# A delta-rule attention with a routed attention behind it, on one core: the first unit's key loads in two pieces, the mask's constants first, 48 small products at the start, and a new order of steps

## The chip, the core and the metric

The kernel runs on one core of a Trainium2 chip. The core has five engines that run side by side, each through its own list of instructions in order: TensorE (PE, matrix products; its weight loads are PEld), VectorE (DVE), ScalarE (ACT), GpSimd (POOL) and SyncE (SP, which here only issues transfers). They wait for one another by semaphores. The metric is the device time of one execution in microseconds (us), from the first to the last instruction, as the median of timed runs.

## The reference

```python
def _attn_ref(q, k, v, beta):                 # 4 batches, 8 heads, 768 tokens, 48 features
    k_n = k / (np.linalg.norm(k, axis=-1, keepdims=True) + 1e-06)
    state = np.zeros((B, H, D, D)); y = np.zeros_like(q)
    for t in range(S):
        kt, vt, bt = (k_n[:, :, t], v[:, :, t], beta[:, :, t, None])
        y[:, :, t] = np.einsum('bhd,bhde->bhe', q[:, :, t], state)
        v_old = np.einsum('bhde,bhd->bhe', state, kt)
        state = state + bt[:, :, :, None] * np.einsum('bhd,bhe->bhde', kt, vt - v_old)
    return y
...
def _moe_ref(x, w_gate, wq, wk, wv, wo):      # x: y as 4 x 768 x 384; 4 experts of width 64, the best 2 count
    logits = x @ w_gate
    ...                                       # w: softmax over the 2 largest logits of a token
    for e in range(E):
        q = x @ wq[e]; k = x @ wk[e]; v = x @ wv[e]
        scores = scale * (q @ k.transpose(0, 2, 1))
        scores = np.where(causal, -1000000000.0, scores)
        a = np.exp(scores - scores.max(-1, keepdims=True))
        a /= a.sum(-1, keepdims=True) + 1e-09
        ye = a @ v @ wo[e]
        ...                                   # out += (w of e, if e is one of the token's two) * ye
```

The recurrence over 768 tokens is the first half, a causal attention of four experts the second.

## The kernel before, in words

The work is cut into six units `n` (two pairs of batches, three thirds of the tokens each). A unit has 256 tokens in four chunks `c` of 64, and eight pairs of heads; the two heads of a pair lie on partitions 0 and 64, the two sides. Units 0 to 2 follow one another for one pair of batches, 3 to 5 for the other.

In a unit each chunk's recurrence becomes a triangular solve. First come the products of K with itself (`gr`, `gram`). `st_in` (`si`) transposes them on DVE, and `pre` (five steps) makes the norms. Then the steps `sv` follow, nearly all of two elementwise instructions: for units 1 to 5 on POOL, 32 steps (L334, L335), for unit 0 on DVE with half the size, 15 steps (L337, L338). `so` and `sn` transpose the result back on DVE. Unit 0's blocks of 16 are then widened to 64 by `dg` (copies on ACT and POOL) and `ex` (four rounds of 32 products for each chunk); its side products are `gu`. Units 1 to 5 widen theirs by `m1`, `mv` and `m2`. `gq` multiplies K and Q, and two DVE instructions copy that out under a mask (L271).

After that each chunk runs a chain: `ks` (K by the state), a subtraction on DVE, `u` (the solved matrix by it), a copy on ACT (L449), `s` (the new state), and for the output `q` and `y`. Pairs of chunks then go through the second half: `hx` (transfers within the core), `pj` and `pv` (projections), `mx`, `mp`, `mr` (row maxima), `sc` (scores and exponentials), `av`, `nm`, `ft`, `fo` (values, output projection, store). `vt` scales V on POOL. `lg`, `lq`, `lc` load K, Q and K/V, `w` loads weights.

The order in which the steps are written is a table, `ORDER`. It lists 854 steps, and each step emits its instructions on all engines at its place; every engine then runs its own part in that order. A number with a plus sign stands for so many fillers: products of zeros on PE, 128 by 256, which nothing reads (`filler`). The products of most steps go to four PSUM banks `pm__66` to `pm__69`, taken in turn, so a step must wait until the bank's last content has been copied out.

At the start PE also runs `MINI` products of 4 columns of zeros, in two records each. The loads are issued by SP in the order of the code: the first K of unit 0, the constants that the first mask needs, the other three K of unit 0, `beta`, the K of unit 1, and so on. A K chunk is 128 rows of 2 KB, of which rows 48 to 63 and 112 to 127 hold zeros and are read by nothing. Transfers take eight semaphores in turn, so the ninth waits until the first has landed.

Of the kernel before, what the change touches and what calls it, by code (L numbers as in the profile page):

```python
# [38 lines left out]
sv0.4 sv0.5 sv0.6 sv0.7 sv0.8 gu1 lc0.1 vt0.1 +16 gu0 sv0.9 vt0.0 ks0.0 +6 gq0.1 +3 gu2 +21 gr1.0 gr1.1 +1 gr1.2
sv0.10 sv0.11 sv0.12 sv0.13 sv0.14 sv0.16 so0 sn0 dg1 si1 pre1.0 gq0.0 lq1.2 dg0 pre1.1 pre1.2 pre1.3 lq1.1 dg2 pre1.4  # L40
sv1.1 +47 ex1.0 +2 gq1.0 ex0.0 kc2 sv1.2 +9 ex1.1 ex0.1 sv1.3 sv1.4 sv1.5 sv1.6 w1 ex2.0 sv1.7 sv1.8 ex1.2 dg3 ex0.2
+7 ex0.3 ex2.1 w3 ex1.3 u0.0 +5 s0.0 gq1.2 w2 sv1.9 sv1.10 ks0.1 y0.0 +1 u0.1 sv1.11 sv1.12 gq0.2 +2 q0.1 s0.1 lc0.2
vt0.2 sv1.13 sv1.14 sv1.15 sv1.16 sv1.17 w0 ex2.2 lc0.3 ex3.0 vt0.3 +6 ex2.3 ks0.2 y0.1 ex3.1 w4 q0.2 sv1.18 u0.2
lq1.3 sv1.19 sv1.20 sv1.21 ex3.2 s0.2 gq0.3 lg2.1 hx0.1.0 ks0.3 sv1.22 sv1.23 sv1.24 lg2.2 sv1.25 lg2.0 y0.2 ex3.3
pv0.0.0 vs1 w5 sv1.26 q0.3 u0.3 lc1.0 gr2.1 gr2.2 y0.3 lg2.3 gr2.3 sv1.27 sv1.28 sv1.29 lq2.1 gr2.0 sv1.30 si2 pj0.0.2
s0.3 hx0.3.0 pj0.0.0 pre2.0 lc1.1 pv0.0.1 pj0.1.0 q1.0 sv1.31 sv1.32 so1 sn1 vt1.0 ks1.0 lg3.0 vt1.1 mv1.3 mv1.0
pj0.1.2 pre2.1 mv1.2 lq2.2 pre2.2 pre2.3 m11.1 m11.0 pv0.1.1 m21.2 +1 m21.0 mv1.1 m21.1 cl1 pre2.4 sv2.1 sv2.2 sv2.3
gq1.1 u1.0 +5 s1.0 sv2.4 mx0.0.0.0 sv2.5 sv2.6 ks1.1 y1.0 u1.1 sv2.7 sv2.8 lc1.2 lq2.0 mx0.0.1.1 q1.1 mp0.0 mx0.1.0.0
s1.1 mr0.0 mx0.1.1.1 vt1.2 mp0.1 ks1.2 y1.1 lc1.3 pv0.1.0 gr3.0 sv2.9 sv2.10 lq2.3 sv2.11 sv2.12 sv2.13 m21.3 u1.2
sv2.14 q1.2 kc0 +1 s1.2 vt1.3 lg3.1 gr3.1 gq2.3 mr0.1 sv2.15 sv2.16 w6 hx1.1.0 sv2.17 +1 sc0.0.1.0 sv2.18 ks1.3 y1.2  # L50
gq1.3 sc0.1.0.0 gt0 sv2.19 q1.3 u1.3 lg3.2 sc0.0.0.0 y1.3 pv1.0.1 lg3.3 gr3.3 s1.3 sv2.20 sv2.21 gr3.2 lc2.0 si3
pre3.0 pv1.0.0 pj1.0.0 vt2.0 pj1.0.2 lq3.0 hx1.3.0 pj1.1.2 sv2.22 sv2.23 vs0 av0.0.3 sv2.24 +3 gq3.0 sv2.25 gq2.1
ks2.0 mx1.0.0.0 sv2.26 sv2.27 pv1.1.1 pre3.1 pre3.2 av0.1.0 sv2.28 pre3.3 av0.0.0 av0.1.1 sv2.29 sv2.30 av0.0.2 sv2.31
sv2.32 av0.0.1 q2.0 mx1.0.0.1 pre3.4 lc2.1 sc0.1.1.0 so2 sn2 sv3.1 pv1.1.0 pj1.1.0 mv2.0 sv3.2 sv3.3 +7 m12.0 m12.1
cl2 nm0.0 +7 m22.0 sv3.4 mx1.1.1.2 vt2.1 av0.1.3 +2 gq2.0 lg4.0 u2.0 sv3.5 mv2.3 sv3.6 mv2.1 lq3.2 lg5.0 mx1.0.1.3
sv3.7 vs2 av0.1.2 s2.0 sv3.8 mx1.1.0.1 ft0.0 ks2.1 m22.1 gq2.2 nm0.1 lg4.1 y2.0 u2.1 sv3.9 mx1.0.1.2 sv3.10 lq3.1
mv2.2 lc2.2 sv3.11 fo0.0.1 mp1.0 fo0.0.0 vt2.2 sv3.12 q2.1 s2.1 sv3.13 m22.2 m22.3 sv3.14 lc2.3 ks2.2 y2.1 sv3.15
sv3.16 sv3.17 ft0.1 mx1.1.1.3 vt2.3 sv3.18 sv3.19 u2.2 mr1.0 q2.2 s2.2 mx1.1.0.0 mp1.1 sc1.0.0.1 sv3.20 sv3.21 sv3.22
gt1 lg4.2 hx2.1.0 fo0.1.1 gr4.2 ks2.3 y2.2 lc3.0 lg4.3 gr4.1 gq3.2 pj2.0.0 q2.3 u2.3 mx2.0.0.0 sv3.23 sv3.24 sc1.0.0.0
y2.3 gr4.3 gr4.0 lc3.1 si4 pre4.0 sv3.25 av1.0.0 av1.0.1 pre4.1 sv3.26 sv3.27 lq4.1 sc1.0.1.0 sc1.0.1.1 pj2.0.2 sv3.28  # L60
pv2.0.1 hx2.3.0 mr1.1 pj2.1.0 sv3.29 sv3.30 pv2.1.1 sv3.31 mx2.0.0.1 lq4.0 av1.0.2 sv3.32 so3 vt3.0 lq3.3 av1.0.3
vt3.1 mv3.3 mv3.1 sc1.1.0.0 sc1.1.0.1 sn3 m13.1 pre4.2 pre4.3 mv3.0 m13.0 ks3.0 cl3 pre4.4 sv4.1 pv2.0.0 sv4.2 sv4.3
sv4.4 av1.1.0 m23.0 m23.1 fo0.1.0 mx2.0.0.2 sv4.5 sv4.6 sv4.7 sv4.8 u3.0 gq4.1 gr5.0 s3.0 pj2.1.2 gq3.1 ks3.1 y3.0
sv4.9 sc1.1.1.0 sc1.1.1.1 lg5.1 sv4.10 u3.1 lc3.2 nm1.0 gq3.3 sv4.11 mv3.2 q3.1 lq4.3 s3.1 mx2.0.1.5 av1.1.1 mx2.0.1.6
mx2.0.1.4 mx2.0.1.7 vt3.2 ks3.2 y3.1 sv4.12 mx2.0.0.3 m23.2 m23.3 sv4.13 sv4.14 ft1.0 sv4.15 pv2.1.0 u3.2 lc3.3 vt3.3
q3.2 lg5.2 mp2.0 mx2.1.1.6 sv4.16 sv4.17 mx2.1.1.5 hx3.1.0 s3.2 av1.1.2 av1.1.3 sv4.18 mr2.0 lq5.0 fo1.0.1 mx2.1.1.4
sv4.19 sv4.20 sv4.21 ks3.3 lg5.3 y3.2 gr5.2 sc2.0.0.2 mx2.1.0.2 sv4.22 q3.3 mx2.1.0.0 sc2.0.0.1 lc4.0 u3.3 sv4.23
# [749 lines left out]
```

## Time and profile before

| | |
|---|---|
| timed runs, median (lowest to highest of 3) | 432.34 us (432.06 to 434.2) |
| the profiled execution, its own time | 431.71 us |
| its span, first to last instruction | 430.0 us |
| PE busy in the span | 406.0 us (94%) |
| POOL busy | 257.2 us (60%) |
| DVE busy | 275.9 us (64%) |
| ACT busy | 202.8 us (47%) |

The profiled execution's own time is 0.6 us under the median of the timed runs. PE's busy time contains the fillers and the small products of zeros; it says how long PE had something in hand, not that the work was useful.

### The profile page before, as it was taken

The page shows a single profiled execution, that of the slowest core. Times are in us where ns is not written, and L with a number is a line of the kernel's source. Part 1 is how long each engine was busy: PE and PEld are TensorE (multiplying, and loading weights), DVE is VectorE, ACT ScalarE, POOL GpSimd, SP SyncE. Part 2 cuts the span into 40 slices and gives each one's busy share as a digit, 9 for nine tenths or more (in the row PEclk, how much of TensorE's full clock was granted, in tenths as well). Part 3 has the DMA queues.
Part 4 walks back from the last instruction along what each step waited for, and adds up shares of the span by engine and source line. Part 5 has one row for each costly group of instructions (what it writes and reads, how often), then busy time and mean ns, then how long its engine had stood idle before and what let it go on. Part 6 is the DMA issues. An engine that isn't in the chain of part 4 may idle for free.

```text
span 430.0 us, 24315 instructions
## 1 busy us (share of the span) xinstructions
PE 406.0 (94%) x10912; PEld 365.6 (85%) x10912; DVE 275.9 (64%) x615; ACT 202.8 (47%) x555; POOL 257.2 (60%) x477
## 2 busy tenths in 40 slices
...
GB/s 252 190 32 99 65 109 174 58 53 109 102 108 40 3 159 121 148 69 5 84 100 117 23 82 6 97 74 57 59 59 42 24 73 47 32 20 22 20 39 74
DMA packets 18967, 32.72 MB, mean 76 GB/s; under 512 B 2864, under 2 KB 9008, under 8 KB 18864
## 3 DMA queue, kind: packets, MB, share of 16 engines
...
## 4 chain that ended last, share of the span: by engine, by line
PE 73%; DVE 13%; POOL 4%; issue 4%; DMA 2%; ACT 1%; SPq 1%; DVEq 0%; ACTq 0%
PE pm__69 L118 15%; PE pm__67 L118 15%; PE pm__68 L118 12%; PE py L118 12%; PE pm__66 L118 11%; PE xu L118 7%; DVE B L278 3%; POOL B L335 2%; POOL tm L334 2%; DVE B L275 1%; DMA kf<-in_kq_dram 1%; DVE tt L355 1%; DVE tn L352 1%; DMA xh<-h 1%; SPq L489 1%
## 5 line engine op out<-in xcount | busy, mean ns | idle before, releaser
L335 POOL TENSOR_TENSOR B<-B,tm 128x30 f32<-128x30 f32 (+9 forms) x150 | 80.7, 538 | 11.8
L334 POOL TENSOR_TENSOR tm<-B 128x30 f32<-128x30 f32 (+9 forms) x150 | 74.1, 494 | 9.9
L642 POOL TENSOR_SCALAR_AFFINE_SELECT at<-at 128x256 f32<-128x256 f32 x48 | 19.1, 409 | 91.8 <-ACT at L640 58.5
L118 PE MATMUL py<-zb 128*128 128x256 bf16 (+1 forms) x256 | 27.1, 264 | 2.7 <-DVE h L483 1.6
L156 POOL TENSOR_TENSOR kv<-kv,nt 128x384 f32<-128x384 f32 x24 | 19.9, 832 | 14.9 <-DVE B L338 11.2
L118 PE MATMUL py<-qf,sb 48*48 48x64 f32 x704 | 24.8, 218 | 2.9 <-issue 1.9
L118 PEld LDWEIGHTS py<-qf,sb 48*48 48x48 f32 x704 | 21.3, 120 | 6.0 <-issue 2.7
L397 POOL COPY tt<-tt 32x256 f32<-32x256 f32 x40 | 15.7, 392 | 11.4 <-DVE tt L355 10.0
L480 ACT ACTIVATE xh<-py 112x384 fp32r<-112x384 f32 x24 | 11.8, 492 | 19.7 <-PE py L118 19.6
L118 PEld LDWEIGHTS <-zb 128*128 128x128 bf16 x176 | 16.5, 103 | 5.2 <-DVE zb L123 1.1
L449 ACT ACTIVATE ub<-xu 128x384 f32<-128x384 f32 x24 | 11.9, 495 | 18.2 <-PE xu L118 13.0
L587 DVE TENSOR_REDUCE mx<-pm__66 128x1 f32<-128x512 f32 (+3 forms) x28 | 17.3, 617 | 4.7 <-PE pm__67 L118 3.2
L118 PE MATMUL pm__67<-xh,wqkh 128*128 128x256 f32 x108 | 19.9, 284 | 0.0
L587 DVE TENSOR_REDUCE mx<-pm__67 128x1 f32<-128x512 f32 (+3 forms) x25 | 16.0, 640 | 5.8 <-PE pm__68 L118 5.8
L482 DVE TENSOR_TENSOR xh<-py,xh 112x384 fp32r<-112x384 f32 x24 | 13.3, 553 | 8.8 <-ACT h L481 8.8
L461 DVE TENSOR_TENSOR sb<-sb,xu 112x384 f32<-112x384 f32 x20 | 11.0, 550 | 10.4 <-PE xu L118 10.3
L118 PE MATMUL pm__67<-kf 48*64 48x64 f32 (+2 forms) x304 | 12.0, 245 | 5.7 <-issue 4.9
L118 PE MATMUL xu<-xs,tt 64*64 64x48 f32 x768 | 16.7, 221 | 0.5 <-DVE xs L443 0.5
L118 PEld LDWEIGHTS xu<-xs,tt 64*64 64x64 f32 x768 | 14.0, 134 | 3.5 <-issue 1.7
L118 PEld LDWEIGHTS pm__67<-xh,wqkh 128*128 128x128 f32 x108 | 16.5, 188 | 0.3 <-DVE QLO L515 0.2
L278 DVE STREAM_TRANSPOSE B<-tt 32x1024 f32<-32x1024 f32 x8 | 16.4, 2045 | 0.2
L118 PEld LDWEIGHTS pm__67<-kf 48*32 48x32 f32 (+1 forms) x304 | 9.6, 140 | 7.7 <-issue 5.5
(359 smaller groups left out, 1621.6 us busy)
## 6 DMA issues: line engine op xcount, KB each, us to landing
...
```

Source lines behind the costliest of these rows:

```text
L118: T.matmul(o, lhsT=a, rhs=b, start=start, stop=stop, skip_group_check=True)
L156: G.tensor_tensor(vt, vt, PR[n]["nt"][:, c * NP:c * NP + NP, None].to_broadcast([128, NP, HD]), op=OP.mult)
L278: V.transpose(B[r:r + 32], gf[r:r + 32, :, 0:32].rearrange("p t j -> p j t"))
L334: e.tensor_tensor(tv, bc(Z[:, i:i + 1, i + 1:]), bc(Z[:, 0:i, i:i + 1]), op=OP.mult)
L335: e.tensor_tensor(Z[:, 0:i, i + 1:], Z[:, 0:i, i + 1:], tv, op=OP.add)
L397: G.tensor_copy(o[r:r + 32, :, 0:32], o[r:r + 32, :, 32:64])
L449: S.activation(eight(UB), PX, AF.Copy)
L461: V.tensor_tensor(eight(new), eight(state(n, c)), SP, op=OP.add)
L480: S.activation(hi, Y[:, :, 0:3], AF.Copy)
L482: V.tensor_tensor(lo, Y[:, :, 0:3], hi, op=OP.subtract)
L587: V.tensor_reduce(dst.rearrange("p (y x) -> p x y", x=2)[:, x, y:y + per], P[x], axis=AX.X, op=OP.max)
L642: G.affine_select(d, d, pattern=[[0, 2], [1, 128]], compare_op=OP.is_ge, fill=0.0, base=0, channel_multiplier=-1)
```

## The change

Four edits, and a new table.

1. The four K chunks of unit 0 are loaded as two transfers of 48 rows each, one a side, without the rows of zeros. SP issues the transfer of side 0 and ACT that of side 1. All other K chunks are loaded as before.
2. The 32 columns of constants that the first mask reads (`kmask`, columns 208 to 239) are a transfer of their own behind the first K; the other 208 columns of that block come after `beta`. The first ACTIVATE (`one`) stands behind the loads of unit 0.
3. `MINI` is 48, not 40.
4. `ORDER` is another order of the same 854 steps, with 166 fillers instead of 175.

```diff
-MINI = 40
+MINI = 48
...
 ORDER = """
-+2 gr0.0 +4 gr0.2 gr0.3 gr0.1 si0 pre0.0 lq1.0 pre0.1 pre0.2 kc1 pre0.3 pre0.4 sv0.1 +4 gr1.3 cb sv0.2 sv0.3 gu3 kc3
...
++11 gr0.0 gr0.1 +4 gr0.3 gr0.2 si0 cb pre0.0 pre0.1 gu1 lq1.0 pre0.2 pre0.3 pre0.4 vt0.0 sv0.1 sv0.2 sv0.3 sv0.4 sv0.5
...
-    S.activation(one, ZB[:, 0:1], AF.Exp)
+
     def load_k(n, c):
         LD[n, c] = KR[(n * CH + c) % KB]
-        nc.sync.dma_start(LD[n, c], kq[n, c][:, 0:NP * 64])
+        if n:
+            nc.sync.dma_start(LD[n, c], kq[n, c][:, 0:NP * 64])
+            return
+
+        for q, r in ((nc.sync, 0), (nc.scalar, 64)):
+            q.dma_start(LD[n, c][r:r + HD], kq[n, c][r:r + HD, 0:NP * 64])
...
     load_k(0, 0)
-    nc.sync.dma_start(cst[:, 0:240], consts[:, 0:240])
+    nc.sync.dma_start(cst[:, 208:240], consts[:, 208:240])
     for c in range(1, CH):
         load_k(0, c)
+    S.activation(one, ZB[:, 0:1], AF.Exp)
     nc.sync.dma_start(bta, beta)
+    nc.sync.dma_start(cst[:, 0:208], consts[:, 0:208])
```

The first place of which the prediction speaks is the start of SP's list. Before, a K chunk is one row (`kf_114` to `kf_117` are unit 0's chunks 0 to 3, `kf_118` is unit 1's first); what an instruction waits for stands in brackets, DMAHW being the transfers' semaphores.

```order
L143 DMA kf_114<-in_kq_dram 128x512
L166 DMA cst<-in_consts_dram 128x240
L143 DMA kf_115<-in_kq_dram 128x512
L143 DMA kf_116<-in_kq_dram 128x512
L143 DMA kf_117<-in_kq_dram 128x512
L169 DMA bta<-in_beta_dram 128x192
L143 DMA kf_118<-in_kq_dram 128x512
```

The same place of the change; here `kf_122` to `kf_125` are unit 0's chunks 0 to 3. ACT's list begins with the other half of each of these four.

```order
L148 DMA kf_122<-in_kq_dram 48x512
L171 DMA cst<-in_consts_dram 128x32
L148 DMA kf_123<-in_kq_dram 48x512
L148 DMA kf_124<-in_kq_dram 48x512
L148 DMA kf_125<-in_kq_dram 48x512 [waits DMAHW0_49]
L175 DMA bta<-in_beta_dram 128x192 [waits DMAHW1_49]
L176 DMA cst<-in_consts_dram 128x208 [waits DMAHW2_49]
L144 DMA kf_126<-in_kq_dram 128x512 [waits DMAHW3_49]
```

SP's half of chunk 3 is the ninth transfer and so waits until one of the first has landed; before, the ninth was unit 1's third chunk.

The second place is DVE behind unit 0's solve. Before, `so0` (`tt_154`) and `sn0` (`tn`) are followed at once by unit 1's `si1` (`B_182`) and `pre1`, with one `gq` (two rows `pm`) in between.

```order
L355 STREAM_TRANSPOSE tt_154<-B_181 128x32x32
L352 STREAM_TRANSPOSE tn<-B_181 128x32x32
L275 STREAM_TRANSPOSE B_182<-tt_155 128x1024
L291 COPY ss<-B_182 128x32
L292 TENSOR_SCALAR g_701<-ss 128x32
L293 TENSOR_SCALAR g_701<-g_701 128x32
L271 TENSOR_TENSOR pm<-pm__69,cst 128x256
L271 TENSOR_TENSOR pm<-pm__66,cst 128x256
L297 RECIPROCAL rr<-g_701 128x32
```

In the change two `gq` (of `gq1.0` and `gq0.3`) stand ahead of `si1` (`B_195`), and a third (`gq0.1`) behind it.

```order
L362 STREAM_TRANSPOSE tt_167<-B_194 128x32x32
L359 STREAM_TRANSPOSE tn<-B_194 128x32x32
L278 TENSOR_TENSOR pm<-pm__67,cst 128x256
L278 TENSOR_TENSOR pm<-pm__68,cst 128x256
L278 TENSOR_TENSOR pm<-pm__69,cst 128x256
L278 TENSOR_TENSOR pm<-pm__66,cst 128x256
L282 STREAM_TRANSPOSE B_195<-tt_168 128x1024
L278 TENSOR_TENSOR pm<-pm__67,cst 128x256
L278 TENSOR_TENSOR pm<-pm__68,cst 128x256
L298 COPY ss<-B_195 128x32
```

The pair of `gq0.1` stood before inside unit 0's solve, between its ninth and tenth step. On PE, `gq0.1` now stands behind 56 fillers and directly ahead of 3 fillers and the first expansion, `ex1.0`; before, 47 fillers stood ahead of `ex1.0`.

## Rows read from the trace of the kernel before

**Rows 1.** Windows: busy us (instructions) of each engine, granted clock, DMA share, GB/s.

```profile
core 0: us, PE busy (x) PEld busy (x) DVE busy (x) ACT busy (x) POOL busy (x), PEclk, DMA share, GB/s
0.00:35.00 35.00, 28.00 (x897) 21.84 (x899) 24.57 (x67) 15.95 (x51) 10.65 (x27) 1.00 0.52 173
...
200.00:425.00 225.00, 222.51 (x5463) 204.27 (x5457) 130.41 (x309) 114.95 (x312) 108.69 (x200) 1.00 0.18 53
...
75.00:80.00 5.00, 5.00 (x121) 4.88 (x110) 2.63 (x3) 2.63 (x8) 4.21 (x13) 0.66 0.10 21
```

**Rows 2.** Timeline of the first 12 us: start, us, engine, instruction, idle before.

```profile
0.82 0.39 SPq L143 DMA_DIRECT2D kf<-in_kq_dram  x1
...
1.14 1.81 PE L118 MATMUL py<-zb 128*128 128x256 bf16 x83 [1.14 <-DVE zb L123]
...
6.85 0.18 PEld L118 LDWEIGHTS pm__69<-kf 48*32 48x32 f32 x5 [1.71 <-DMA kf<-in_kq_dram]
...
7.59 0.23 PEld L118 LDWEIGHTS pm__67<-kf 48*32 48x32 f32 x8
...
9.53 0.18 PEld L118 LDWEIGHTS pm__69<-kf 48*32 48x32 f32 x5
```

**Rows 3.** The K tiles to 30 us: time from issue to landing, eight loads.

```profile
DMA to landing us min/median/max: 2.9/5.2/6.3
```

**Rows 4.** The chain that ended last, to 110 us: start, us, what.

```profile
17.71 3.30 PE py L118 x16
...
29.55 5.24 PE py L118 x47
34.79 1.08 PE pm__67 L118 x32
...
39.90 0.93 PE pm__68 L118 x32
...
47.45 0.45 PE xu L118 x28
...
72.61 2.08 issue
```

**Rows 5.** Timeline of DVE, from unit 0's products to unit 1's `so`.

```profile
10.94 1.90 DVE L275 STREAM_TRANSPOSE B<-tt 128x1024 f32<-128x1024 f32 x1
...
23.13 0.42 DVE L271 TENSOR_TENSOR pm<-pm__67,cst 128x256 f32<-128x256 f32 x1
23.47 0.41 DVE L271 TENSOR_TENSOR pm<-pm__68,cst 128x256 f32<-128x256 f32 x1
...
27.42 2.04 DVE L355 STREAM_TRANSPOSE tt<-B 128x1024 f32<-128x1024 f32 x1
29.35 1.91 DVE L352 STREAM_TRANSPOSE tn<-B 128x1024 f32<-128x1024 f32 x1
...
33.04 0.39 DVE L291 COPY ss<-B 128x32 f32<-128x32 f32 x1
...
37.40 0.19 DVE L305 SCALAR_TENSOR_TENSOR nn<-rr,bta 128x32 f32<-128x32 f32 x1
...
40.05 0.69 DVE L379 TENSOR_TENSOR VS<-tt,pm__67 128x512 f32<-128x512 f32 x1 [1.69 <-PE pm__67 L118]
...
87.85 2.08 DVE L355 STREAM_TRANSPOSE tt<-B 128x1024 f32<-128x1024 f32 x1
```

**Rows 6.** Timeline of POOL: `dg` copies, unit 1's solve from L308 to L348.

```profile
32.63 0.39 POOL L364 COPY VS<-tn 32x256 f32<-32x256 f32 x1
...
37.74 2.35 POOL L308 TENSOR_TENSOR B<-B,nn 128x1024 f32<-128x1024 f32 x1 [1.25 <-DVE aa L312]
...
48.30 0.30 POOL L363 MEMSET tt<- 32x256 f32 x1
...
82.88 0.24 POOL L348 COPY B<-aa 128x32 f32<-128x32 f32 x1
```

**Rows 7.** Timeline of ACT: the copies behind `u4.0` and `u4.3`.

```profile
264.69 0.53 ACT L449 ACTIVATE ub<-xu 128x384 f32<-128x384 f32 x1
...
305.21 0.49 ACT L449 ACTIVATE ub<-xu 128x384 f32<-128x384 f32 x1 [1.95 <-issue]
```

More of the change, by code (lines that the diff above doesn't have):

```diff
@@ L37 @@
 ORDER = """
-+2 gr0.0 +4 gr0.2 gr0.3 gr0.1 si0 pre0.0 lq1.0 pre0.1 pre0.2 kc1 pre0.3 pre0.4 sv0.1 +4 gr1.3 cb sv0.2 sv0.3 gu3 kc3
[L39 to L67, printed above, removed]
@@ L88 @@
-fo5.0.1 ft5.1 +12 fo5.1.0 fo5.1.1
++11 gr0.0 gr0.1 +4 gr0.3 gr0.2 si0 cb pre0.0 pre0.1 gu1 lq1.0 pre0.2 pre0.3 pre0.4 vt0.0 sv0.1 sv0.2 sv0.3 sv0.4 sv0.5
+sv0.6 sv0.7 sv0.8 +11 gr1.2 sv0.9 +14 gr1.1 sv0.10 gu3 gu0 +5 gu2 kc3 lc0.1 vt0.1 gr1.3 sv0.11 sv0.12 sv0.13 sv0.14
+sv0.16 so0 sn0 +3 gr1.0 dg1 gq1.0 gq0.3 dg0 si1 +56 gq0.1 +3 ex1.0 pre1.0 pre1.1 pre1.2 dg2 +10 ex0.0 pre1.3 dg3 gq0.0
+lq1.2 pre1.4 +9 ex0.1 sv1.1 sv1.2 sv1.3 sv1.4 sv1.5 ex1.1 ks0.0 +1 ex0.2 w4 ex2.0 sv1.6 ex3.0 ex0.3 sv1.7 w5 w1 ex2.1
@@ new lines @@
+sv1.8 sv1.9 sv1.10 u0.0 ex1.2 sv1.11 s0.0 ex1.3 ks0.1 y0.0 lc0.2 vt0.2 lg2.1 sv1.12 sv1.13 ex2.2 lq1.1 sv1.14 sv1.15
+lg2.0 u0.1 q0.1 s0.1 w2 +6 ks0.2 kc1 sv1.16 ex2.3 y0.1 lc0.3 ex3.1 vt0.3 gr2.1 w3 q0.2 u0.2 w0 +5 s0.2 hx0.1.0 sv1.17
+gq0.2 lg2.2 ks0.3 sv1.18 sv1.19 sv1.20 ex3.2 sv1.21 y0.2 sv1.22 sv1.23 sv1.24 sv1.25 +1 ex3.3 kc2 q0.3 vs0 pv0.0.0
+gr2.0 u0.3 gq1.2 y0.3 lg2.3 gr2.3 w6 sv1.26 vs1 gr2.2 s0.3 si2 pj0.0.0 hx0.3.0 pj0.0.2 sv1.27 sv1.28 pv0.0.1 lc1.0 kc0
+sv1.29 sv1.30 pre2.0 +1 pj0.1.0 q1.0 sv1.31 lc1.1 sv1.32 so1 vt1.0 ks1.0 vt1.1 mv1.3 mv1.2 sn1 pre2.1 pj0.1.2 pv0.1.1
```

62 lines of the change are left out of this document (42 added, 20 removed).

## The prediction

> **What bounds the kernel now.** I read the windows first, to see where PE has no room. From 200 us on it is busy 222.5 of 225 us: whatever is late or early there is PE's own queue, and a shift that reaches this stretch comes out at the end at full size. In the first 35 us it is busy 28.0 us, and much of that is fillers [rows 1]. So the change can win ahead of 200 us only, and it touches the first 35 us most. Then I read the timelines of the start. PE waits for K: the second group of products of unit 0 starts at 6.85 us, after a wait for the transfer [rows 2]. DVE can transpose those products at 10.94 us and from there runs unit 0's solve almost without a pause, to `so0` at 27.42 and `sn0` at 29.35 us [rows 5]. Last the chain: up to 34.79 us it runs through fillers, 47 of them in one piece from 29.55 us, and then the first expansion `ex1.0` begins [rows 4]. Its data were there earlier: the last copy that it needs, POOL's second of `dg1`, ended at 32.63 + 0.39 = 33.02 us [rows 6]. So 1.8 us of those fillers are too many. From the expansions the chain goes on PE to unit 0's first chain product at 47.45 us [rows 4], and unit 1's `so1` on DVE at 87.85 us comes 4.7 us after POOL had solved unit 1, at 82.88 + 0.24 = 83.12 us [rows 5, 6]. DVE was behind in its list by then, and the last entry ahead of `so1` copies out a projection of PE. Up to there the pace is PE's, not POOL's.
>
> **The start (edits 1, 2, 3).** PE's first 83 products (80 records of small ones, three of full size) take 1.81 us, to 2.95 us [rows 2]. A full one costs 3.30/16 = 0.206 us at the slower level of PE's clock (256 columns in that time is 1.2 GHz) and 5.24/47 = 0.111 us at the faster [rows 4]; so a small record is (1.81 - 3 x 0.206)/80 = 0.015 us, and the 16 more of edit 3 cost 0.24 us. Nine more fillers ahead of the first products, at the slow level, cost 1.85 us. PE is there at 5.04 us. The first K, issued at 0.82 us, had landed after 2.9 us, at 3.7 us [rows 2, 3], and is smaller now, so nothing waits. A group of a chunk's products takes 7.59 - 6.85 = 0.74 us; three groups and four fillers later, at 8.1 us, the fourth begins. From the fourth group to the transpose it was 10.94 - 9.53 = 1.41 us [rows 2, 5]. The transpose then stands at 9.5 us, 1.45 us earlier. Bounds: at the fast level of the clock from the start it would be 1.5 us earlier still (13 fillers, 0.095 each, and part of the groups). On the other side, SP's half of chunk 3 is the ninth transfer and leaves only when the first has landed, at 3.7 us. With the shortest landing it is there at 6.6 us, before its group (7.3 us); with the longest, 6.3 us [rows 3], at 10.0 us, which puts the transpose at 12.2 us, 1.2 us later than before. I take no wait, because a quarter of the bytes ahead of it is gone and the constants that used to go in between are a seventh. ACT's four issues hide: it does nothing else before 12 us that anyone waits for.
>
> **Unit 0's solve to the expansions (edit 4).** The pair of `gq0.1` leaves the solve: 2 x (23.47 - 23.13) = 0.68 us [rows 5]. `so0` comes 2.1 us earlier, `sn0` ends at 29.1 instead of 31.26 us, and the copies of `dg1` at 30.9. `gq0.1` on PE needs the banks of `gq1.0`, which DVE empties right behind `sn0`, at 29.8 us; its 32 records take no longer than an expansion's 32, 0.93 us [rows 4], and three fillers 0.33 us. So `ex1.0` begins at about 31.0 instead of 34.79 us: 3.8 us. Here 2.1 us come from the earlier solve and the rest from fillers that no longer overrun. For PE's own list this is late enough: 92 fillers and eleven groups from 8.9 us on end at 8.9 + 92 x 0.111 + 11 x 0.74 = 27 us, or 31 us if the first 40 run at the slow level.
>
> **Expansions to the first chain.** DVE is now the one that is late: from 29.1 us it runs two pairs for `gq` (1.36), `si1` (1.90), a third pair (0.68), `pre1` (33.04 to 37.59 before, less the pair within: 3.87) and a fourth pair (0.68), and reaches the first subtraction of an expansion at 37.7 us, against 40.05 us [rows 5]. PE has `ex0.1` ready at 36.8 us (ex1.0, 10 fillers, `ex0.0`, `gq0.0`, 9 fillers) and would reach `ex0.2`, which needs that subtraction, at 37.9 us; it waits until 38.4. Five expansions at 0.93 us bring `u0.0` to 43.1 us. Before, 47.3: **4.2 us earlier**. This is the sum's main term; of it DVE already takes 0.5 us back.
>
> **POOL.** Unit 1's solve starts when `nn` is there, at 37.0 instead of 37.74 us, only 0.7 us earlier. But the four copies of `dg3` stood inside the solve (48.30 us on) and stand ahead of it now: 2 x (0.30 + 0.39) = 1.4 us. So the solve ends at 81.0 us [rows 6], and `so1`, shifted with PE by 4.2 us, is wanted at 83.65. POOL keeps 2.6 us of room, and unit 2's solve gets PE's whole shift.
>
> **The rest of the order.** Behind `u0.3` there are 27 fillers instead of 39, 1.3 us less. I count nothing for them: the ones that went stood where PE waits for unit 2's solve, and a wait takes their place. The last 12 fillers stay. The useful products are the same, and from 200 us on the shift stays what it is.
>
> **The sum.** 431.71 - 4.2 = 427.5 us for the profiled execution, and 0.6 us more for the median of timed runs: **428.1 us**.
>
> **The rivals.** *The shift is eaten on the way* (no change, 430.2 to 434.5). One way: somewhere before 100 us PE waits for a solve, and then only POOL's 2.1 us count; another pause like the 2.08 us at 72.61 us, after which the granted clock is 0.66 from 75 to 80 us (1.7 us lost at half level) [rows 1, 4], leaves 0.4 us: 431.9 us. For it: the fillers before `gq0.1` may run out 2.8 us before DVE frees the bank. Against: one such pause is in the kernel before too. Another way is the split: if the halves of chunk 3 land in 6.3 us, DVE starts 1.2 us late, `so0` comes at 28.0 us, and the first expansion gains 1.1 us by the overrun alone: 431.2 us. The Trainium skill speaks for this one (DMA: Bandwidth & Descriptors, "Rules for kernel authors"): two transfers to disjoint halves of the partitions share the same engines, so splitting a load gains nothing. By that rule the pieces only add transfers that take turns at the semaphores; no row here shows a split load, and against it stands that the rows of zeros could go in no other way.
>
> *Slower* (over 434.5 us): unit 4's chain. In the new table `u4.0` stands later, and between it and `u4.3` stand 35 steps with products instead of 45, some 30 us of PE's work instead of 40 (the sums of these steps' durations in the trace). The chain takes turns with DVE, ACT and POOL; before, it was spread over 305.21 - 264.69 = 40.5 us [rows 7]. If it needs all of that, PE stands 10.5 us in a stretch that has no room: 438.6 us. It decides from a wait of 6.4 us on. Against it: 40.5 us was the spacing of the old table, and unit 0's chain began at 47.45 us and was at its fourth chunk before the pause at 72.61 us [rows 4], some 8 us a chunk.
>
> *More than forecast* (under 425 us): the 1.3 us of fillers and the 1.7 us of slow clock come out as well: 425.1 us and less.
>
> **How the numbers follow.** Forecast (425 to 430.2): 0.56. More: 0.08. Eaten: 0.22. Slower: 0.14. A measurement of this kernel tells 0.5% (2.2 us) from no change. So faster 0.64, same 0.22, slower 0.14. The range leaves out the slower rival and the far end of more: 424.5 to 434.5 us. The forecast's own range is 425 to 430.2 us.
>
> **What would show it.** Right: DVE's first transpose at 9 to 10 us, `so0` at 25 to 26 us, the first expansion at 30.5 to 31.5 us, the first subtraction at 37 to 38.5 us, `u0.0` at 42.5 to 44 us, `so1` before 84.5 us, and PE over 98% busy from 195 us on. Wrong at the start: PE idle in front of chunk 3's products. Wrong in the middle: a granted clock under 1 between 25 and 45 us, or DVE reaching `so1` at once behind POOL. Wrong in the end: gaps of PE between `u4.0` and `u4.3`. What would make the number wrong most easily is a wait between 85 and 200 us, where the whole order is new and I have priced it as before.

## The result: 1.1% slower, and the profile after

| | before | after |
|---|---|---|
| timed runs, median (lowest to highest) | 432.96 us (432.06 to 434.2, 4 runs) | 439.61 us (436.58 to 440.9, 4 runs) |
| ratio to before, 95% interval | | 1.0108 [1.0064, 1.0152] |
| the profiled execution, its span | 431.71, 430.0 us | 436.58, 434.7 us |

The forecast was 428.1 us, with a range of 424.5 to 434.5. The ratio on record is not the quotient of the two medians, which is 1.015; how it was formed is not part of the record. The profiled execution is the fastest of the four after, so its trace shows 4.7 us of loss in the span where the medians differ by 6.7. Runs more than 1.5% above the fastest of their kernel count as slow and are left out of the ratios; the traces of e1 and h3 further down are of such runs.

Windows of the kernel after, against [rows 1]; the last is a stretch at half clock:

```profile
0.00:35.00 35.00, 28.64 (x931) 22.51 (x935) 21.90 (x63) 13.10 (x44) 9.15 (x22) 1.00 0.40 130
200.00:425.00 225.00, 221.87 (x5422) 202.52 (x5417) 132.77 (x321) 113.84 (x310) 109.69 (x201) 1.00 0.17 51
...
95.64:105.88 10.24, 9.35 (x284) 8.57 (x282) 6.82 (x14) 2.98 (x8) 8.50 (x17) 0.50 0.25 81
```

The landing of unit 0's halves of K, against [rows 3], the timeline of PE at the fourth group of products (`gr0.2`), against [rows 2], and the first piece of the chain that has no cause, against [rows 4]:

```profile
DMA to landing us min/median/max: 2.7/3.3/4.8
```

```profile
12.82 0.21 PE L118 MATMUL pm__66<-kf 48*32 48x32 f32 x1 [3.49 <-issue]
```

```profile
9.33 3.49 issue
...
28.78 0.70 issue
29.48 5.18 PE py L118 x46
...
35.72 1.08 PE pm__69 L118 x32
```

K was there, as forecast: SP's last half was issued at 3.7 us, and PE's waits up to 14 us name no transfer of K. But inside `gr0.2`, with nothing to wait for that the profile names, PE stands for 3.49 us. DVE, against [rows 5] (its lines are now 7 higher: L282 is `si`, L362 `so`, L386 the subtraction), and POOL, against [rows 6]:

```profile
13.23 0.29 DVE L257 TENSOR_TENSOR tt<-pm__69,cst 128x128 f32<-128x128 f32 x1 [3.95 <-PE pm__66 L118]
...
13.75 1.94 DVE L282 STREAM_TRANSPOSE B<-tt 128x1024 f32<-128x1024 f32 x1
...
29.66 1.98 DVE L362 STREAM_TRANSPOSE tt<-B 128x1024 f32<-128x1024 f32 x1
...
41.85 0.69 DVE L386 TENSOR_TENSOR VS<-tt,pm__69 128x512 f32<-128x512 f32 x1 [0.40 <-PE pm__69 L118]
...
87.66 2.08 DVE L362 STREAM_TRANSPOSE tt<-B 128x1024 f32<-128x1024 f32 x1
```

```profile
34.82 0.39 POOL L371 COPY VS<-tn 32x256 f32<-32x256 f32 x1
...
42.02 2.37 POOL L315 TENSOR_TENSOR B<-B,nn 128x1024 f32<-128x1024 f32 x1
...
86.11 0.24 POOL L355 COPY B<-aa 128x32 f32<-128x32 f32 x1
```

So DVE begins 2.8 us later than before instead of 1.45 earlier, `so0` comes at 29.66, `ex1.0` at 35.7, and `u0.0` at 47.53 us (47.23 before by the same view, the timeline of PE; 43.1 forecast). The late solve is not all of it: the data of `ex1.0` were there at 34.82 + 0.39 = 35.21 us, and PE came 0.44 us later, straight out of its own products and fillers.

Yet that is not the loss either. When DVE transposes unit 3's solution (`so3`), the two kernels are nearly level (before, then after):

```profile
195.99 2.04 DVE L355 STREAM_TRANSPOSE tt<-B 128x1024 f32<-128x1024 f32 x1
...
195.83 2.05 DVE L362 STREAM_TRANSPOSE tt<-B 128x1024 f32<-128x1024 f32 x1
```

By equal work PE is then 0.9 us behind (an estimate, from the sum of the steps' usual durations in the traces). Most of the 4.7 us come later. From unit 3's first `m1` product to the start of its second `s` (`s3.1`) the kernel before takes 17.03 us (198.41 to 215.44), the one after 22.02 (198.03 to 220.05). By the same estimate 2.1 us more of products stand in that stretch in the new table, and 2.9 us are lost. Of these the windows show 1.5 us as idle time of PE; the rest is spread over steps that take longer than usual there. Windows of before, then of after:

```profile
200.00:210.00 10.00, 10.00 (x305) 9.23 (x298) 3.67 (x14) 6.91 (x16) 8.96 (x17) 1.00 0.08 25
210.00:220.00 10.00, 10.00 (x399) 9.07 (x398) 8.26 (x18) 4.29 (x13) 9.00 (x18) 1.00 0.42 136
```

```profile
200.00:210.00 10.00, 9.48 (x282) 8.79 (x276) 9.00 (x29) 6.83 (x16) 9.00 (x16) 1.00 0.01 4
210.00:220.00 10.00, 9.04 (x247) 7.64 (x241) 8.00 (x21) 3.41 (x10) 6.95 (x14) 1.00 0.22 70
```

DVE is busy 9.00 us of ten instead of 3.67. Its timeline after shows with what: the gates of unit 1 (`gt1`, L548 to L565) and `nm1.0` (L668 to L672) stand there now, and behind them the copies (L278) that free the banks for PE. Nearly half of the time of `gt1` is one small instruction, `gd`, which ends 0.03 us behind a multiplication on POOL, the first row here (`pre4.4`).

```profile
204.30 2.38 POOL L315 TENSOR_TENSOR B<-B,nn 128x1024 f32<-128x1024 f32 x1
204.44 2.27 DVE L549 TENSOR_TENSOR gd<-lg,gm 128x16 f32<-128x16 f32 x1
...
209.63 0.74 DVE L672 TENSOR_TENSOR on<-os,rs 128x512 f32<-128x512 f32 x1
210.30 0.36 DVE L319 TENSOR_TENSOR aa<-rr,bta 128x32 f32<-128x32 f32 x1
210.57 0.41 DVE L278 TENSOR_TENSOR pm<-pm__69,cst 128x256 f32<-128x256 f32 x1
```

PE waited for that copy, in the table of waits from 199 to 212 us:

```profile
PE pm__69 L118 <- DVE pm L278: 0.9, 1, 0.9
```

Between 250 and 270 us both kernels stand, in different places. The one after stands 0.83 us at 262.23, for a copy behind `so4`, and 0.37 at 270.01, for an instruction behind `gt2` and `nm2.0`; the one before stands 1.41 us at 251.28, for a copy behind `pre5.1`. Where the last 0.9 us of the 4.7 are lost these rows don't show. The rival that I had for slower, unit 4's chain, is not it. From the copy behind `u4.0` to that behind `u4.3` it now takes 30.2 us, against 40.5 in [rows 7]:

```profile
277.55 0.49 ACT L456 ACTIVATE ub<-xu 128x384 f32<-128x384 f32 x1 [0.36 <-PE xu L118]
...
307.79 0.49 ACT L456 ACTIVATE ub<-xu 128x384 f32<-128x384 f32 x1 [1.67 <-PE xu L118]
```

### The profile page after: what moved, and what is told of

Same layout as the page of the kernel before. It is cut to its first block, busy times and chain, and to the rows that moved or that the text cites. A ratio compares the mean times of both kernels' runs of the same rounds, so it can differ in the third digit from the quotient of the medians.

```text
span 434.7 us, 24380 instructions
## 1 busy us (share of the span) xinstructions
PE 410.6 (94%) x10919; PEld 370.1 (85%) x10919; DVE 276.4 (64%) x615; ACT 203.6 (47%) x555; POOL 257.6 (59%) x477
## 3 DMA queue, kind: packets, MB, share of 16 engines
q1 hardware_dynamic: 18688, 30.52, 22.3%
## 4 chain that ended last, share of the span: by engine, by line
PE 76%; DVE 13%; issue 4%; POOL 2%; ACT 2%; DMA 1%; SPq 1%; DVEq 0%; ACTq 0%; POOLq 0%
PE pm__68 L118 15%; PE pm__67 L118 15%; PE pm__66 L118 13%; PE pm__69 L118 13%; PE py L118 12%; PE xu L118 7%; DVE B L285 2%; DVE mx L594 1%; DVE B L282 1%; DVE tn L359 1%; PE pm__69 L681 1%; DMA xh<-h 1%; SPq L496 1%; DVE g L300 1%; POOL B L342 1%
## 5 line engine op out<-in xcount | busy, mean ns | idle before, releaser
L118 PE MATMUL py<-zb 128*128 128x256 bf16 (+1 forms) x263 | 26.2, 261 | 3.4 <-DVE h L490 1.6
L118 PE MATMUL pm__68<-xh,wqkh 128*128 128x256 f32 x144 | 27.2, 288 | 0.0
L404 POOL COPY tt<-tt 32x256 f32<-32x256 f32 x40 | 15.8, 395 | 12.2 <-DVE tt L362 4.0
L118 PEld LDWEIGHTS pm__68<-xh,wqkh 128*128 128x128 f32 x144 | 21.9, 188 | 0.6
L594 DVE TENSOR_REDUCE mx<-pm__69 128x1 f32<-128x512 f32 (+3 forms) x28 | 17.5, 627 | 5.5 <-PE pm__66 L118 3.1
L118 PE MATMUL pm__68<-xh,wqkl 128*128 128x256 f32 x72 | 20.1, 279 | 0.0
L594 DVE TENSOR_REDUCE mx<-pm__67 128x1 f32<-128x512 f32 (+3 forms) x20 | 12.1, 606 | 11.4 <-PE pm__68 L118 9.9
L118 PE MATMUL xu<-xs,tt 64*64 64x48 f32 x768 | 17.9, 226 | 0.4
L594 DVE TENSOR_REDUCE mx<-pm__66 128x1 f32<-128x512 f32 (+3 forms) x27 | 16.7, 618 | 1.9 <-PE pm__67 L118 1.9
L118 PE MATMUL xu<-sb,kf 48*64 48x48 f32 x704 | 15.7, 226 | 2.2 <-issue 1.1
L118 PEld LDWEIGHTS xu<-sb,kf 48*64 48x64 f32 x704 | 13.0, 138 | 4.8 <-DVE sb L468 2.1
L456 ACT ACTIVATE ub<-xu 128x384 f32<-128x384 f32 x24 | 11.9, 494 | 10.7 <-PE xu L118 9.0
```

Source lines behind the costliest of these rows:

```text
L118: T.matmul(o, lhsT=a, rhs=b, start=start, stop=stop, skip_group_check=True)
L404: G.tensor_copy(o[r:r + 32, :, 0:32], o[r:r + 32, :, 32:64])
L456: S.activation(eight(UB), PX, AF.Copy)
L594: V.tensor_reduce(dst.rearrange("p (y x) -> p x y", x=2)[:, x, y:y + per], P[x], axis=AX.X, op=OP.max)
```

## The experiments

Two things were to be told apart: the start (with its pause), and the new order behind it. Each ratio is against runs of the kernel before on the same chip; times in us are of the profiled execution. "351st" is when PE starts its 351st product, "m1 to s" the stretch from unit 3's first `m1` to `s3.1`. The medians of the kernel before were 433.0 to 435.9 us on the chips of these runs, 0.7% apart; late times of two traces can therefore differ by about 1 us without any edit (an estimate: 0.7% of 196 us is 1.4 us). Diffs show parts of lines where a line of the table is long.

| kernel | ratio [95%] | 351st | si0 | ex1.0 | u0.0 | m1 to s |
|---|---|---|---|---|---|---|
| before | 1 | 14.65 | 10.94 | 34.72 | 47.23 | 17.0 |
| after | 1.0108 [1.0064, 1.0152] | 12.82 | 13.75 | 35.65 | 47.53 | 22.0 |
| e1_mini24 | 1.0232 [1.0179, 1.0286] | 14.31 | 10.27 | 37.87 | 49.74 | 22.4 |
| e2_loads_only | 1.0070 [1.0036, 1.0103] | 14.29 | 10.59 | 37.38 | 49.89 | 17.0 |
| e3_order_only | 1.0173 [1.0121, 1.0226] | 13.35 | 14.28 | 35.57 | 47.57 | 22.0 |
| e4_start_oldtail | 1.0093 [1.0057, 1.0128] | 14.14 | 10.60 | 38.27 | 50.15 | 17.0 |
| f1_mini48_alone | 1.0163 [1.0104, 1.0223] | 13.15 | 13.92 | 38.22 | 50.73 | 17.0 |
| f2_short_opening | 1.0263 [1.0205, 1.0322] | 13.60 | 10.92 | 37.04 | 48.91 | 24.8 |
| f3_oldstart_newtail | 1.0249 [1.0193, 1.0305] | 14.23 | 11.72 | 35.73 | 48.24 | 22.0 |
| f4_newstart_oldtail | 1.0215 [1.0163, 1.0268] | 13.14 | 14.07 | 36.26 | 48.43 | 17.1 |
| g1_mini32 | 0.9977 [0.9939, 1.0014] | 14.85 | 11.00 | 34.18 | 46.69 | 17.1 |
| g2_31_fillers | 0.9965 [0.9937, 0.9993] | 15.46 | 12.56 | 33.75 | 47.26 | 17.1 |
| g3_mini48_31_fillers | 1.0038 [1.0007, 1.0070] | 13.03 | 13.80 | 35.70 | 48.43 | 17.0 |
| g4_short_opening_16_fillers | 1.0142 [1.0095, 1.0189] | 14.46 | 11.24 | 32.48 | 44.48 | 22.3 |
| h1_fillers_in_waits | 1.0145 [1.0101, 1.0188] | 12.89 | 13.76 | 35.48 | 47.36 | 22.6 |
| h2_newstart16_oldtail | 1.0122 [1.0084, 1.0160] | 13.47 | 9.97 | 31.21 | 43.20 | 17.7 |
| h3_mini43 | 1.0042 [1.0006, 1.0078] | 14.24 | 9.85 | 37.31 | 49.83 | 17.0 |
| h4_mini44 | 1.0092 [1.0056, 1.0128] | 13.43 | 14.00 | 36.85 | 49.36 | 17.0 |
| i1_31_fillers_no_single | 0.9952 [0.9931, 0.9973] | 15.63 | 11.44 | 34.86 | 47.37 | 17.0 |
| i2_mini32_31_fillers_no_single | 1.0072 [1.0036, 1.0108] | 15.76 | 11.87 | 34.08 | 46.99 | 20.0 |

**The opening (e1), and the parts alone (e2, e3).** e1 is the kernel after with one number changed:

```diff
-MINI = 48
+MINI = 24
```

> The kernel after with 24 opening py products instead of 48, nothing else. In the kernel before TensorE stands 2.77 us with no wait (11.87 to 14.65 us, inside gr1.3), in the one after 3.49 us (9.33 to 12.82, inside gr0.2), both times at about the 350th matmul of the program. Theory A (the stall sits at a place of the instruction stream, and the longer opening moved it into the first unit's last K product): with 48 records fewer gr0.2 ends before 9.6 us, si0 starts before 10.0 (13.75 in the kernel after), u0.0 at 43.7 to 44.5 (47.5); a stall of about 3 us comes some 48 records later, in or behind gu1. The total then gains 2 to 4 us, 433 to 438, if the rest of the order costs what it did. Theory B (the stall comes from K, the banks or the clock): it stays inside gr0.2 and si0 stays at 13 us or later; total 438 to 441. If the start is mended and the total stays at 438 or more, the order behind the start holds most of the loss.

The pause moved to `gu1`, as theory A had it, and DVE began at 10.27 us; but `ex1.0` came 2.2 us later than in the kernel after. Its data were there at 31.5 us (POOL's second copy of `dg1`); PE's own list, 56 fillers in it, held it until 37.9. Theory A was right on the pause and wrong on what follows from it.

e2 is before with the new loads (edits 1 and 2; the diff shows the first); e3 is after with the old loads.

```diff
...
-        nc.sync.dma_start(LD[n, c], kq[n, c][:, 0:NP * 64])
+        if n:
+            nc.sync.dma_start(LD[n, c], kq[n, c][:, 0:NP * 64])
+            return
+
+        for q, r in ((nc.sync, 0), (nc.scalar, 64)):
+            q.dma_start(LD[n, c][r:r + HD], kq[n, c][r:r + HD, 0:NP * 64])
...
```

> The kernel before with the changed loads alone (K's halves by two queues without zero rows, the mask's constants ahead); 40 opening products and the old order. Theory A (loads harmless, the loss is of the order and of where the stall falls): the 350th record stays inside gr1.3, si0 starts 1 to 2.5 us earlier than before's 10.94, total 430 to 433. Rival (two queues and the earlier DMA issues on ScalarE cost later work, or the halves land late): total 435 or more. If the old order cannot use the earlier start, 432 to 434 and u0.0 within 0.5 us of before's 47.3.

> The kernel before with the new order and 48 opening products, K loaded whole with its zero rows by one queue as before. Theory A: the stall of about 3 us still falls at the 350th record, inside gr0.2 or near it, si0 at 13.5 to 14.5 as in the kernel after, and the total is that of the kernel after, 437 to 441: the loads bought nothing because the stall ends later than any chunk of K lands. Rival (the new loads carry the loss): 434 or less. If K's later arrival adds to the stall instead of lying beside it: si0 at 15 or later, 441 to 444.

In the old order the loads do not gain: `ex1.0` is 2.7 us later than before, and the total 0.7% longer. PE waited 1.72 us for the last chunk's ninth transfer (to 8.36 us), but that isn't what made `ex1.0` late, for DVE still began 0.35 us earlier than before. Inside the solve DVE then stood 2.91 us for the products of `gq0.1`, to 25.73 us; in h3, which has the old loads, it stands there for 2.78. With the new order and the old loads (e3) `u0.0` comes at 47.57 us, with the new ones at 47.53: up to there the loads bought nothing.

**Where PE pauses (f1, h3, h4).** The windows count PE's products, as records of the trace: a product of `MINI` and most others leave two, a filler one. Up to the pause and up to its end, for the kernel after:

```profile
0.00:9.36 9.36, 7.89 (x350) 5.84 (x351) 1.63 (x7) 2.49 (x4) 6.02 (x16) 1.00 0.60 180
0.00:12.80 12.80, 7.89 (x350) 5.84 (x351) 1.63 (x7) 2.49 (x4) 6.02 (x16) 1.00 0.66 203
```

and for the kernel before, where the pause lies in `gr1.3`, of which nobody is in need:

```profile
0.00:11.90 11.90, 7.65 (x350) 5.26 (x350) 3.08 (x10) 1.49 (x2) 6.01 (x16) 1.00 0.80 266
0.00:14.60 14.60, 7.65 (x350) 5.26 (x350) 5.54 (x17) 1.79 (x3) 6.01 (x16) 1.00 0.85 288
```

Both stop at 350 products, with quite different work. Unit 0's four K groups end at product 343 before and at 368 after. f1 changes the opening alone, h3 and h4 are one product of the opening apart, two records (groups ending at 349 and 351):

```diff
-MINI = 40
+MINI = 48    # f1; h3: 43; h4: 44
```

> The kernel before with 48 opening products for 40, nothing else (edit 3 alone). In all six traces so far TensorE pauses at the same counts of matmuls, 223 and 350 (then 605, 732, 859), whatever stands there, and each pause ends 1.2 to 1.6 us after a transfer of 16 KB on the instruction queue has landed. Theory A (its instructions come in blocks of 127 matmuls, and a block that it reaches too early is waited for): in the kernel before unit 0's four K groups end at count 343, with 48 openings at 359, so the last nine products of gr0.1 wait for the block behind 350. si0 starts at 12.5 to 14.5 us (10.94 before), u0.0 at 48 to 50 (47.3), total 1 to 3 us more than before. Rival (16 small products cost only their own 0.24 us, and the stall belongs to gr1.3 or to the loads): si0 within 0.5 us of 10.94, total within 0.5 us of before.

> The kernel before with 43 opening products for 40. Unit 0's four K groups end at count 349, one ahead of the block end at 350. Block theory: si0 within 0.8 us of before's 10.94 or up to 12.6 as it varied (10.9 to 12.6 in four runs of that start), no pause inside gr0.1, total within 0.7% of before. Rival (the cost grows with each product of the opening): si0 and the total a third of the way to the kernel with 48, that is +1 us and +2.5 us.

> One opening product more than 43: the K groups end at count 351, so the last product of gr0.1 stands behind the block end at 350. Block theory: a pause of 2.5 to 4 us in front of that one product, si0 at 13 to 14.3, 2 to 3 us later than with 43, total 2 to 7 us over the one with 43. Rival: no more than 0.3 us later than with 43 at si0 and in total.

Timeline of h3, then of h4: the product of PE behind the pause, and DVE's `si0`.

```profile
14.24 0.80 PE L118 MATMUL py<-zb 128*128 128x256 bf16 x3 [4.54 <-issue]
...
9.85 1.90 DVE L275 STREAM_TRANSPOSE B<-tt 128x1024 f32<-128x1024 f32 x1
```

```profile
13.43 0.21 PE L118 MATMUL pm__66<-kf 48*32 48x32 f32 x1 [3.67 <-issue]
...
14.00 1.97 DVE L275 STREAM_TRANSPOSE B<-tt 128x1024 f32<-128x1024 f32 x1
```

With 43 the pause falls on a filler, with 44 on the last K product: 4.15 us at `si0` for one product of 4 columns. That shows that the count sets the place. All 20 traces pause at 350 (0.85 to 4.78 us), and none starts its 351st product before 12.82 us (12.82 to 15.76). But the totals of h3 and h4 aren't clearly apart (1.0042 and 1.0092, intervals that overlap; 2 to 7 us were expected). `ex1.0` comes at 37.31 and 36.85, with its data there at 34.61 and 35.95 us: what PE still has to do behind the pause, fillers included, sets it, not the solve. f1 has the same `si0` as h4 and costs more, 1.6%: its `u0.0` is 1.4 us later, the rest comes behind.

**The count behind the start (g1, g2, g3).** g1 is the control with 32 opening products (`MINI`); g2 takes 16 of the 47 fillers out; g3 does so with 48 opening products, so that all later products have the numbers that they had before.

```diff
-+47 ex1.0
++31 ex1.0
```

> The kernel before with 32 opening products for 40: the control for the 48 alone. Unit 0's K groups end at count 327, the block behind 350 again begins inside gr1.3. Theory A (what matters is that the K groups stay ahead of count 350): si0 within 0.6 us of 10.94, u0.0 within 1 us of 47.3, total within 0.7% of before. Rival (any change of the count is as bad, since all 85 block ends behind it then fall on other products, or the shorter opening costs clock): 438 us or more.

> The kernel before with 31 fillers for 47 ahead of the first expansion. The data of ex1.0 are there at 33.0 us, TensorE reaches it at 34.79. Theory (TensorE's fillers set the first expansion): ex1.0 at 33.0 to 33.3, u0.0 at 45.3 to 46.2 (47.3 before), and the total 1 to 2 us lower than before if nothing behind takes it back. Rival (the 16 products fewer move every later block end, and the waits at 50 to 75 us with the clock behind them come out otherwise): total within 1 us of before or over it, though u0.0 is earlier.

> The kernel before with 48 opening products and 31 fillers for 47: the 16 products more at the start are taken out ahead of ex1.0, so that behind it every block of instructions ends where it did in the kernel before. si0 at 13 to 14.5 as with 48 alone. Theory 1 (of the loss of 48 alone the part behind the start is the shift of the later block ends): ex1.0 at 36 to 36.7, u0.0 at 48.5 to 49.5, total 1 to 3 us over before. Theory 2 (the part behind the start comes from the late start itself, waits and clock): total 5 us or more over before, as with 48 alone.

Eight opening products fewer change nothing, so it is not every change of the count that costs. g2 is 0.35% faster, though its pauses fell worse and `u0.0` is where it was; why isn't shown. g3 takes three quarters of f1's loss back (1.0163 to 1.0038): `u0.0` 2.3 us earlier, the rest behind it. Whether that rest is the realigned count or the earlier start isn't separated by these runs.

**A mended start (f2, g4), and the two halves crossed (f3, f4, e4, h2).** f2 brings the K groups of the kernel after back to 343; g4 cuts its fillers too; h2 puts the old sequence behind g4's `u0.0`.

```diff
-MINI = 48
+MINI = 40
...
-+11 gr0.0
++2 gr0.0
...
-si1 +56 gq0.1
+si1 +16 gq0.1    # g4 and h2
```

> The kernel after with 40 opening products for 48 and 2 leading fillers for 11: unit 0's K groups end at count 343 again, ahead of 350; loads and the rest of the new order stay. Theory A: no pause of 3 us inside gr0.2, the one at 223 stays; si0 at 10 to 11 us (13.75 in the kernel after). If the solve is what sets the first expansion, u0.0 at 44 to 45 us. If TensorE's own list does (its fillers, slower while its clock is low, as with 24 openings), ex1.0 at 35 us or later though its data are there by 32.5, and u0.0 at 47 to 50: the start then brings nothing, and the total stays at 436 to 441.

> The kernel after with 40 opening products, 2 leading fillers for 11 (as in the short opening before) and 16 fillers for 56 ahead of gq0.1 and ex1.0. With the short opening alone the data of ex1.0 were there at 32.4 us and TensorE came at 37.04. Theory (TensorE's own list of fillers set the first expansion there): ex1.0 at 32.5 to 34, u0.0 at 44 to 45.8, the earliest of all runs. If the early start holds to the end, total 4 us under the short opening (446) or better. If the sequence behind and the half clock hold the loss: u0.0 early, total still 437 or more.

> New loads and the new order up to u0.0 in the mended form (40 opening products, 2 leading fillers for 11, 16 for 56), behind u0.0 the old sequence. With the new sequence behind it this start had u0.0 at 44.5 us, 2.7 earlier than before, and still 6 us more in total. Theory (the new sequence behind u0.0 loses it): u0.0 at 44 to 45.5, total 429 to 433, at or under before. Rival (the loss is in what an early start meets, whatever the sequence: POOL's solves, block ends, clock): 436 or more.

f2: `si0` at 10.92, `ex1.0` at 37.04 us, its second case; the data were there at 32.35. g4 and h2 then do what I had forecast of the change, `u0.0` at 44.48 and 43.20 us. Neither ends under before. g4 and the kernel after have the same sequence behind `u0.0`. Timelines of g4: PE at `u0.0`, DVE at unit 1's and unit 3's `so`.

```profile
44.48 0.68 PE L118 MATMUL xu<-xs,tt 64*64 64x48 f32 x32
...
85.97 2.07 DVE L362 STREAM_TRANSPOSE tt<-B 128x1024 f32<-128x1024 f32 x1
...
196.05 2.06 DVE L362 STREAM_TRANSPOSE tt<-B 128x1024 f32<-128x1024 f32 x1
```

At `u0.0` g4 is 3.05 us ahead of the kernel after, at `s0.3` 2.75 (74.49 against 77.24), at `so1` 1.7, at unit 2's first `m1` product 0.55 (146.25 against 146.80), and at `so3` it is 0.2 behind. h2 has the sequence of before, but is a weaker trial than its `u0.0` suggests. It is 4.0 us ahead there, and at `s0.0` level (48.54 us in both kernels): where the tables meet, two expansions that stood ahead of `u0.0` stand behind it, and PE stands twice for 0.89 us. What it has in hand is other work done early (`ex3.0`, `gq0.3`), and from there it is 0.9 us ahead at `s0.3` (79.41 against 80.29), 0.3 at unit 2's first `m1` (146.65 against 146.93), and 0.8 behind at `so3`. And it paused 2.39 us inside `y0.3`, without a cause that the profile names, with half clock from 75.5 to 78.9 us after it:

```profile
74.34 0.31 PE L118 MATMUL py<-pm,ub 64*48 64x64 f32 x2 [2.39 <-issue]
```

> The kernel before (old loads, 40 openings, old order up to u0.0) with the new sequence behind u0.0. u0.0 at 47 to 48 us as before. Theory A2 (the new sequence behind u0.0 loses 3 to 5 us by itself: more waits between 60 and 100 us, a longer half clock, the waits at 207 to 212 and 260 to 268 us): 435.5 to 439. Rival (the sequence behind u0.0 is neutral, the loss is all of the start): within 1.5 us of before.

> The kernel after (new loads, 48 openings, new order up to u0.0, the pause inside gr0.2 with it) with the old sequence behind u0.0. u0.0 at 47 to 48.5 us. Theory A2: within 1.5 us of before, as u0.0 stands where it stood and the old sequence follows. Rival (the start carries the loss): as the kernel after, 437 to 441.

f3 and f4 are slower than either parent, so the totals of crossed tables don't split the loss. Nor does e4, the new start with 24 opening products ahead of the old sequence: expected at 428 to 433 us if the new sequence alone were at fault, it took 438.71 (1.0093). The stretch at unit 3 separates the sequences: 17.0 to 17.7 us in twelve of the thirteen kernels with the old one behind `u0.0` (20.0 in i2, with half clock inside), 22.0 to 22.4 in five of the seven with the new one (24.8 in f2 and 22.6 in h1, with half clock inside). Some 2.1 us of the difference are the products that moved there (the estimate above).

**The clock (h1).** In the kernel after, taken out or filled where PE stood between 65 and 100 us:

```diff
-+1 ex3.3
+ex3.3
...
-+2 m21.0
++6 m21.0
...
-s1.0
+s1.0 +8
```

> The kernel after, start and all, with three edits between 65 and 100 us, where TensorE stood: the single filler behind y0.2 taken out (it waited 1.58 us until DVE had read the py tile that fillers share with y), 6 fillers for 2 ahead of m21.0 (TensorE waited 0.51 us there), 8 fillers behind s1.0 (it waited 0.89). Theory (TensorE's idle stretches between 55 and 100 us are what the granted clock of 0.5 from 95.64 to 105.88 us follows, and that stretch costs 5 us): the half clock behind 90 us is gone or shorter, total 2 to 5 us under the kernel after, 433.5 to 436 against before's 433. Rival (the clock falls all the same, or the fillers only delay): within 1.5 us of the kernel after, 438 or more.

The stretch at 95 us is gone, others are there (windows of h1), and the total is no better than that of the kernel after (1.0145 and 1.0108, intervals overlapping): the rival holds. As h1 has more time at half clock than the kernel after (13.6 us in these windows against 10.24), it doesn't show what the slow clock is worth.

```profile
64.20:67.60 3.40, 3.40 (x90) 2.71 (x88) 1.62 (x2) 1.87 (x4) 3.24 (x5) 0.50 0.19 39
125.70:132.50 6.80, 6.52 (x108) 6.29 (x109) 4.07 (x3) 2.31 (x8) 6.09 (x13) 0.50 0.35 92
204.20:207.60 3.40, 3.40 (x44) 3.34 (x38) 2.55 (x8) 1.40 (x3) 2.91 (x5) 0.50 0.02 5
```

By chance h1 also bears on the stretch at unit 3. POOL's multiplication ends there 0.08 us after `gd` has begun, and `gd` takes 0.17 us. The wait of PE for the copy behind the gates, 0.92 or 0.93 us in the other six kernels with the new sequence, is 0.28 us:

```profile
210.29 0.17 DVE L549 TENSOR_TENSOR gd<-lg,gm 128x16 f32<-128x16 f32 x1
...
215.07 0.50 PE L118 MATMUL pm__69<-KHI,QHI 64*128 64x512 f32 x1 [0.28 <-DVE pm L278]
```

**A version that beats both (i1, i2).** g2 without the single filler behind `y0.0`, which waits for DVE to read `py`; i2 has 32 opening products as well.

```diff
-y0.0 +1 u0.1
+y0.0 u0.1
```

> The kernel before with 31 fillers for 47 ahead of ex1.0 and without the single filler behind y0.0, which waits until DVE has read py (50.85 to 52.42 us in the kernel before, while the data of u0.1 are there at 51.45). With 31 fillers alone: 0.35% under before. If the 1 us that u0.1 then comes earlier holds to the end: 0.5 to 0.7% under before, about 431 against 433.5. Rival (TensorE between 50 and 80 us is held by the rate at which its blocks of instructions come, no two transfers of them closer than 3.3 us in any trace, so an earlier u0.1 waits later): no better than the 31 fillers alone.

> The same with 32 opening products for 40, 16 matmuls fewer ahead of everything. If the number of matmuls is what the start and the stretch to 80 us pay for: 0.3 to 0.6% under the version with 40 openings. Rival (the later rise of the clock takes it back): within 0.2% of it.

i1 takes 433.26 us against 435.93 on that chip; by the ratio on record that is 0.48% less. It isn't clearly better than g2 (0.9965, the intervals overlap), so what the single filler is worth isn't shown. PE waits 0.65 us at `u0.1` instead of 1.57 at the filler. i2 starts as hoped (`u0.0` 46.99, `m12.0` at 146.6 us) and loses behind 147 us, with half clock three times between 151 and 271 us; why it and not i1 stays open.

## Why the prediction was wrong

- **The start term** failed at "nothing waits", which held for K alone. Its parts were right: PE reached the first group at 4.93 us (5.04 forecast), the fourth at 8.6 (8.1), K in time. The pause of 3.49 us at product 351 was not in it, and `si0` at 13.75 us lay outside my bounds (8.0 to 12.2). The trace of before held it: 2.77 us of the same kind in `gr1.3`, between two rows that I quoted. Since it lay on a product that nobody needed I didn't ask what sets its place; 16 records and nine fillers more moved it onto one that DVE needs.
- **The solve** was sized right: 15.9 us from `si0` to `so0` (15.8 forecast). So was the way from `ex1.0` to `u0.0` (11.9; 12.1).
- **PE's own list ahead of `ex1.0`**, which I took to end at 27 or 31 us and so never to matter, ended at 35.65 in the kernel after, with three stops without a named cause in it (3.49 us, 0.54 to 25.46 and 0.70 to 29.48). So even a solve in time would have left `ex1.0` there. The same list sets it in e1, f2 and h3, where the data were there 2.7 to 6.4 us before PE came. I had allowed for the slow clock in one bound and for no stop.
- **POOL's solve of unit 1** was sized right: 44.3 us from 42.02 to 86.35 (44.0 forecast). It began 5 us later than forecast, 4.3 us of which is the late `so0`.
- **Unit 2's solve "gets PE's whole shift"**: shown wrong by g4. With nearly the start that I forecast, it is 3.05 us ahead of the kernel after at `u0.0`, 0.55 at 147 us, and not at all at `so3`, 196 us. So the number would have been wrong without the pause too; up to there it is the rival *eaten on the way*. Which wait takes how much of the lead isn't settled (g4 loses it step by step from 74 us on), nor why h2, with the old sequence, ends 1.2% over before.
- **The rest of the order**, of which I had written that "I have priced it as before", was named as the likeliest error and was it. The place I named (85 to 200 us) ended 0.9 us behind; 2.9 us more were lost from 198 to 220 us, in the stretch from which I had said that "the shift stays what it is" (both are estimates by equal work). That all seven kernels with the new sequence are slower there is shown. That `gt1` and `nm1.0` on DVE are the cause is read from the rows: h1, where `gt1` was short, has a third of the wait for the copy behind them, but no kernel moved them alone.
- **Slower** had the right sign by another mechanism; its own, unit 4's chain, went 10 us faster than before. The rule on split loads (Trainium skill, DMA: Bandwidth & Descriptors, "Rules for kernel authors") is neither borne out nor refuted: the halves landed in a median of 3.3 us and the whole chunks before in 5.2, but they also carry fewer bytes. In the kernel after no wait for them is left on PE; the ninth transfer cost PE 1.72 us in e2.
